# Products of P and V issued as two column halves of 64 queries by turns, and eight constants moved to another PSUM bank

## The chip, the cores and the metric

One core of a Trainium2 chip runs one program. Its engines work side by side and wait for each other by semaphores: TensorE (PE; its weight loads are listed apart as PEld), VectorE (DVE), ScalarE (ACT), GpSimd (POOL) and SyncE (SP), which issues most transfers. The metric is the device time of one execution in microseconds; lower is better.

## What is computed

Attention that keeps the 32 largest scores of each query, then a routed feed-forward layer with 8 experts, then a dense one with g = h cos(h). Cut to what matters here:

```python
# q, k, v: (4, 8, 576, 64) fp32
scores = np.matmul(q, k.transpose(0, 1, 3, 2)) / np.sqrt(D)
kth = np.partition(scores, -32, axis=-1)[..., -32:-31]
scores = np.where(scores >= kth, scores, -1e9)
attn = np.exp(scores - scores.max(-1, keepdims=True))
attn = attn / (attn.sum(-1, keepdims=True) + 1e-9)
x = np.matmul(attn, v)                      # the products of P and V
x = x.transpose(0, 2, 1, 3).reshape(2304, 512)
x = moe(x)      # top tokens of each expert by capacity 288, relu(x w1) w2
out = (h * cos(h)) @ w_out                  # h = x @ w_in
```

## The kernel before

Attention is 144 tiles of 128 queries by 576 keys: for each of 16 pairs of heads, four full tiles of each head and a ninth tile (`hs == 2`) that holds the last 64 queries of both heads. Four tiles are a group; there are 36 groups. `run` is a software pipeline written out by hand: in `step`, group gA = step gets its scores (`qk_mm` on PE, `qk_ev` on ACT writes `S`), gB its largest values by chunks (`chunks`, `thresh` on DVE), gC its sign count and exponentials (`sign_exp` on ACT: `sg`, `E`) and the product `W` (`below` on POOL), gD its 32nd largest score (`kth` on DVE) and the masked exponentials `P` (`probs`, on DVE, ACT and POOL by a pattern of four letters), gE the transposes of P (`tr`, `tr_tail` on PE; copies `PT` and `PTt` on ACT), gF the products with V (`av`), gG the division (`fin` on DVE). Each engine does its instructions in the order in which this loop writes them; a letter `u` counts the four tiles of a group.

`kth` takes the eight largest of `W` and picks the one whose rank was counted: four instructions a step (`oh`, L241) that compare the count with `R8`, eight constants for all partitions that stand in PSUM. `tr_tail` (L283) transposes the last 64 keys of two tiles into `ptail`, and one ACT copy a group (L293, `PTt`) takes them out. In `tight` steps, the last ones, copies and products come one tile at a time.

`av` computes out[queries, 65] = P^T-blocks times V with a column of ones: four blocks of 128 keys (L308) and one of the last 64 keys, which are stored for two heads together (L309). The stationary operand is the transposed P, 128 keys by 128 queries; what streams are the 65 columns of V. In fp32 the chip shows two instructions for each product. In ordinary steps `av` is called for two tiles when u = 2 and for two when u = 3; this is called a visit below. For the ninth tile it already computes two halves of 64 queries, all of the first and then all of the second.

The eight PSUM banks hold two `sp` tiles of two banks, two `pt`, one `av` and one `ptail`. Before, the bank `av` is one tile for the whole stage (`B2`); it holds the products (columns 0 to 259) and `R8` (260 to 267). Waits are set by tile: whoever touches a tile waits for the others who touched it before.

After attention comes the routing search, then the gathers, the two feed-forward layers and the stores.

Of the kernel before, what the change touches and what calls it, by code (L numbers as in the profile page):

```python
# [9 lines left out]
F32 = mybir.dt.float32  # L10
# [83 lines left out]
def head_tiles():  # L94
    t = []
    for p in range(NP):
        for s in range(2):
            for i in range(4):
                t.append((p, s, i))
        t.append((p, 2, 4))  # L100
    return t
# [11 lines left out]
class Attention:  # L113
# [4 lines left out]
    def __init__(s, k, sb, ps, slow=False):  # L118
        s.k, s.nc, s.sb, s.ps, s.slow = k, k.nc, sb, ps, slow
        s.tiles = head_tiles()  # L120
        s.nsp, s.ntail = (1, 2) if slow else (2, 1)
        G = s.nc.gpsimd

        s.B2 = ps.tile([128, 512], F32, name="av")
        s.R8 = s.B2[:, 260:268]
        s.nc.vector.tensor_copy(s.R8, k.rank8)

        s.XB, s.XT = {0: s.x_tile()}, {0: s.x_tile(0)}
        s.NV = 2 if slow else 6
        s.VM = [sb.tile([128, 2, 4, 65], F32, name=f"vm{i}") for i in range(s.NV)]  # L130
        s.VT = [sb.tile([128, 2, 2, 65], F32, name=f"vt{i}") for i in range(s.NV)]
        for t in s.VM:
            G.memset(t[:, :, :, 64:65], 1.0)
        for t in s.VT:
            for z in range(2):
                G.memset(t[64 * z:64 * z + 64, z, :, 64:65], 1.0)
                G.memset(t[64 * (1 - z):64 * (1 - z) + 64, z], 0.0)
        s.QZ = []
        for i in range(1 if slow else PLACES):
            z = [sb.tile([128, 512], F32, name=f"qz{i}{a}") for a in range(2)] + [sb.tile([128, 128], F32, name=f"qm{i}")]  # L140
            G.memset(z[0][64:128, :], 0.0)
            G.memset(z[1][0:64, :], 0.0)
            G.memset(z[2][0:64, 64:128], 0.0)
            G.memset(z[2][64:128, 0:64], 0.0)
            s.QZ.append(z)
        s.QT, s.KT, s.SP, s.SS, s.CC, s.TB, s.NMX, s.SUM, s.M3 = ({} for _ in range(9))
        s.todo, s.turned = [], []
        s.SG, s.EX, s.W, s.TB2, s.PB, s.PT, s.PTL, s.PTS, s.AVP = ({} for _ in range(9))
# [130 lines left out]
    def tr_tail(s, j):  # L279
        g, u = divmod(j, 4)  # L280
        if u == 1:
            s.PTL[g] = s.ps.tile([128, 2, 128], F32, name="ptail", bufs=s.ntail)
        s.nc.tensor.transpose(s.PTL[g][:, u // 2, :], s.PB[j // 2][:, 512:640], s.k.ident)  # L283

    def tr_ev(s, j):
# [9 lines left out]
    def av(s, j, two=False):  # L295
        PEe = s.nc.tensor
        g, u = divmod(j, 4)
        p, hs, i = s.tiles[j]
        t, tt = s.values(p)
        if u == 0:  # L300
            if two and g % 2 == 0:
                s.AVP[g] = s.ps.tile([128, 2, 512], F32, name="sp", bufs=s.nsp)[:, 0, :260].rearrange("p (a b) -> p a b", a=4)
            else:
                s.AVP[g] = s.B2[:, :260].rearrange("p (a b) -> p a b", a=4)
        o = s.AVP[g]
        for a, lo, hi in (((hs, 0, 128),) if hs < 2 else ((0, 0, 64), (1, 64, 128))):
            for c in range(4):
                PEe.matmul(o[lo:hi, u, :], s.PT[j][:, c * 128 + lo:c * 128 + hi], t[:, a, c, :], start=c == 0, stop=False)  # L308
            PEe.matmul(o[lo:hi, u, :], s.PTS[g][:, u // 2, lo:hi], tt[:, j % 2, a, :], start=False, stop=True)  # L309

    def fin(s, g, ends):
# [1232 lines left out]
```

## Time and profile before

| | |
|---|---|
| median of 3 runs | 1247.97 us (1246.42 to 1253.18) |
| the profiled execution | 1246.51 us, its span 1244.7 us |
| PE busy | 1131.7 us, 91% of the span |
| DVE busy | 1058.9 us, 85% |
| ACT busy | 787.8 us, 63% |
| POOL busy | 603.3 us, 48% |
| mean granted TensorE clock | 0.948 of full speed |

Busy time is the time in which an engine had an instruction under way. Matmuls are pipelined, so a busy PE is not PE at its peak. A row of a timeline gives the start in us from the span's start, the time until the end of the last instruction in the row, the engine, the line, what is written and read, the shapes (for PE first the rows and columns of the array in use), the count, and in brackets the idle time before it and who ended it.

### The profile page before, as it was taken

How to read it: one execution, taken by the hardware profiler on the slowest of the kernel's cores; microseconds unless marked ns; L12 is line 12 of the kernel's file. 1: busy time of each engine (PE TensorE's matmuls, PEld its weight loads, DVE VectorE, ACT ScalarE, POOL GpSimd, SP SyncE). 2: the span in 40 equal slices, each digit the busy share in tenths (PEclk: the TensorE clock that was granted, in tenths of full speed). 3: DMA queues.
4: the chain of work that ended last, by engine and by line, in shares of the span. 5: the costliest groups of instructions: out<-in, count | busy, mean ns of one | idle time of the engine just before them, and what ended most of it. 6: DMA issues, size and time to landing. Idle time of an engine off the chain costs nothing.

```text
span 1244.7 us, 22829 instructions
## 1 busy us (share of the span) xinstructions
PE 1131.7 (91%) x7449; PEld 996.6 (80%) x7449; DVE 1058.9 (85%) x4172; ACT 787.8 (63%) x1539; POOL 603.3 (48%) x592
## 2 busy tenths in 40 slices
PE   6799999999999986688898989989889999999996
PEld 4588787787878776578888889978777998999985
DVE  7999999999999984687888878699999668777774
ACT  6999989989998951333445446655655545444442
POOL 5999989989998960211000020164665343121120
PEclk9999999989998986698999989999898999999998
DMA  5111121121111001455555567522321100000000
GB/s 124 38 45 38 38 70 32 32 70 32 32 32 39 2 1 39 155 171 164 189 175 167 172 197 240 178 68 85 130 93 67 35 26 18 26 26 27 26 26 29
DMA packets 61890, 98.07 MB, mean 79 GB/s; under 512 B 30912, under 2 KB 30912, under 8 KB 61248
## 3 DMA queue, kind: packets, MB, share of 16 engines
q1 hardware_dynamic: 53648, 74.47, 19.6%
q10 hardware_dynamic: 5136, 12.60, 3.0%
q0 software_dynamic: 2976, 9.44, 2.3%
q8 instruction: 61, 1.00, 0.3%
q14 instruction: 69, 0.57, 0.1%
HBM read 78.66 MB, written 17.83 MB: 78 GB/s over the span
## 4 chain that ended last, share of the span: by engine, by line
PE 36%; DVE 32%; ACT 13%; issue 9%; POOL 5%; DMA 4%; POOLq 0%; DVEq 0%; SPq 0%; ACTq 0%
PE pa L1326 10%; PE y L1374 10%; DVE C L195 5%; PE pa L1174 4%; PE y L1189 4%; ACT sg L226 4%; DMA row<-x,i 3%; DVE w L244 3%; ACT E L228 3%; ACT S L189 2%; DVE wu L1256 2%; PE sp L185 2%; ACT PT L287 2%; PE av L308 2%; DVE ct L1334 2%
## 5 line engine op out<-in xcount | busy, mean ns | idle before, releaser
L1326 PE MATMUL pa<-yh,wu 128*128 128x384 f32 x1152 | 222.3, 340 | 10.7 <-POOL yh L1310 4.8
L1374 PE MATMUL y<-wu,gh 128*128 128x512 f32 x864 | 222.7, 402 | 5.6 <-POOL gh L1362 4.9
L1326 PEld LDWEIGHTS pa<-yh,wu 128*128 128x128 f32 x1152 | 206.0, 189 | 22.4 <-POOL yh L1310 6.4
L232 POOL TENSOR_TENSOR W<-sg,S 128x576 f32<-128x576 bf16 x144 | 197.8, 1379 | 33.0 <-ACT sg L226 31.6
L1374 PEld LDWEIGHTS y<-wu,gh 128*128 128x128 f32 x864 | 164.2, 192 | 38.9 <-POOL gh L1362 6.5
L185 PE MATMUL sp<-kT,qz 128*128 128x288 f32 x512 | 175.7, 433 | 12.7 <-ACT S L189 7.4
L195 DVE MAX8 C<-S 128x8 f32<-128x72 f32 x1152 | 162.5, 215 | 6.5 <-ACT S L189 6.3
L308 PE MATMUL av<-vm,PT 128*128 128x65 f32 (+1 forms) x1216 | 150.5, 274 | 13.7 <-DVE xb L331 7.5
L308 PEld LDWEIGHTS av<-vm,PT 128*128 128x128 f32 (+1 forms) x1216 | 139.1, 190 | 20.4 <-DVE xb L331 11.4
L1358 ACT ACTIVATE gh<-cx 128x384 fp32r<-128x384 f32 x95 | 49.9, 525 | 143.4 <-DVE cx L1356 140.9
L1151 POOL DMA_INDIRECT row<-x,i x24 | 29.5, 1231 | 215.9 <-DVE hh L1181 34.4
L269 POOL TENSOR_TENSOR P<-sg,E 128x576 f32<-128x576 bf16 x102 | 131.4, 1288 | 3.8
L1174 PE MATMUL pa<-xh,wu 128*128 128x288 f32 x768 | 124.9, 314 | 0.0
L277 PEld LDWEIGHTS pt<-ident,P 128*128 128x128 f32 x576 | 80.2, 145 | 52.7 <-POOL P L269 11.5
L1189 PE MATMUL y<-hh,wu 128*128 128x288 f32 x768 | 120.1, 306 | 0.0
L277 PE MATMUL pt<-ident,P 128*128 128x128 f32 x576 | 110.7, 279 | 6.0 <-POOL P L269 4.6
L1174 PEld LDWEIGHTS pa<-xh,wu 128*128 128x128 f32 x768 | 112.1, 201 | 3.2 <-issue 2.9
L226 ACT ACTIVATE sg<-S,tb 128x576 bf16<-128x576 f32 x144 | 111.7, 775 | 1.2
L228 ACT ACTIVATE E<-S,nmx 128x576 f32<-128x576 f32 x144 | 110.8, 769 | 0.0
L1189 PEld LDWEIGHTS y<-hh,wu 128*128 128x128 f32 x768 | 109.2, 196 | 1.7 <-ACT hh L1180 0.8
L189 ACT ACTIVATE S<-sp 128x576 f32<-128x576 f32 x144 | 92.5, 642 | 27.8 <-PE sp L185 27.7
L244 DVE MAX8 w<-W 128x8 f32<-128x576 f32 x144 | 104.6, 746 | 1.3 <-POOL W L232 1.2
(243 smaller groups left out, 2149.8 us busy)
## 6 DMA issues: line engine op xcount, KB each, us to landing
raw<-in_moe_w_dram SPq DMA_DIRECT2D x63, 512.0 KB, 3.9
kT<-in_k_dram SPq DMA_DIRECT2D x16, 288.0 KB, 3.2
qz<-in_q_dram SPq DMA_DIRECT2D x32, 128.0 KB, 3.2
vm<-in_v_dram SPq DMA_DIRECT2D x32, 128.0 KB, 3.0
x<-xb SPq DMA_DIRECT2D x4, 1024.0 KB, 4.1
r<-in_moe_w_in_dram ACTq DMA_DIRECT2D x8, 512.0 KB, 4.9
r<-in_moe_w_out_dram ACTq DMA_DIRECT2D x8, 512.0 KB, 5.0
half<-in_moe_w_in_dram SPq DMA_DIRECT2D x8, 512.0 KB, 3.7
```

The lines of the kernel that those rows point to most:

```text
L185: s.nc.tensor.matmul(s.SP[j][:, c, :288], lh, s.KT[p][:, o + c * 288:o + c * 288 + 288], start=True, stop=True)
L195: s.nc.vector.max(c[:, e, :], s.SS[j][:, 72 * e:72 * e + 72])
L226: A.activation(s.SG[j], s.SS[j], AF.Sign, bias=s.TB[g][:, u:u + 1], scale=-EPS1, accum_out=s.SUM[g][:, u:u + 1])
L228: A.activation(s.EX[j], s.SS[j], AF.Exp, bias=s.NMX[g][:, u:u + 1])
L232: s.nc.gpsimd.tensor_tensor(s.W[j], s.SG.pop(j), s.SS[j], op=OP.mult)
L244: V.max(w8[:, u, :], s.W.pop(4 * g + u))
L277: s.nc.tensor.transpose(s.PT[j][:, i * 128:(i + 1) * 128], s.PB[j // 2][:, o + i * 128:o + (i + 1) * 128], s.k.ident)
L308: PEe.matmul(o[lo:hi, u, :], s.PT[j][:, c * 128 + lo:c * 128 + hi], t[:, a, c, :], start=c == 0, stop=False)
L1174: PEe.matmul(p, w[:, a, f * 128:(f + 1) * 128], XH[e, c][:, b, :], start=n == 0, stop=n == 11)
L1189: PEe.matmul(Y[e][m], w[:, a, o + m * 128:o + (m + 1) * 128], t[:, b, :], start=f == 0 and i == 0, stop=f == 7 and i == 2)
L1326: s.nc.tensor.matmul(p, w[:, a, f * 128:(f + 1) * 128], s.YH[q, c][:, b, :], start=n == 0, stop=n == 11)
L1374: PEe.matmul(O[q][m], g[:, a, m * 128:(m + 1) * 128], w[:, b, c:c + 512], start=first and j == 0, stop=last and j == 2)
```

## The change

Every tile's products are now issued as two halves of 64 queries (columns of the stationary operand), by turns: block c of the first half, block c of the second, then block c + 1. The ninth tile, whose halves belong to two heads, gets the same order. The products get a tile of their own from the pool (`av`), and `R8` moves to a tile for the whole stage (`B1`) that also holds the transposes of the last keys (`ptail`, columns 0 to 255). The count of banks is the same.

```diff
-        s.nsp, s.ntail = (1, 2) if slow else (2, 1)
+        s.nsp = 1 if slow else 2
...
-        s.B2 = ps.tile([128, 512], F32, name="av")
-        s.R8 = s.B2[:, 260:268]
+        s.B1 = ps.tile([128, 512], F32, name="ptail")
+        s.R8 = s.B1[:, 256:264]
...
         if u == 1:
-            s.PTL[g] = s.ps.tile([128, 2, 128], F32, name="ptail", bufs=s.ntail)
+            s.PTL[g] = s.B1[:, :256].rearrange("p (a b) -> p a b", a=2)
...
             else:
-                s.AVP[g] = s.B2[:, :260].rearrange("p (a b) -> p a b", a=4)
+                s.AVP[g] = s.ps.tile([128, 4, 65], F32, name="av")
         o = s.AVP[g]
-        for a, lo, hi in (((hs, 0, 128),) if hs < 2 else ((0, 0, 64), (1, 64, 128))):
-            for c in range(4):
+
+        halves = tuple((hs if hs < 2 else z, 64 * z, 64 * z + 64) for z in range(2))
+        for c in range(4):
+            for a, lo, hi in halves:
                 PEe.matmul(o[lo:hi, u, :], s.PT[j][:, c * 128 + lo:c * 128 + hi], t[:, a, c, :], start=c == 0, stop=False)
+        for a, lo, hi in halves:
             PEe.matmul(o[lo:hi, u, :], s.PTS[g][:, u // 2, lo:hi], tt[:, j % 2, a, :], start=False, stop=True)
```

The program's order on PE in an ordinary step, third tile of a group (u = 2), before. The number behind a tensor's name is one of its buffers; the brackets name the engines waited for.

```order
L283 MATMUL ptail<-ident,P 128x128 [waits Activation_49]
L185 MATMUL sp<-kT,qz_177 128x288 [waits Activation_49]
L277 MATMUL pt<-ident,P 128x128 [waits Activation_49,Pool_49]
L277 MATMUL pt<-ident,P 128x128
L185 MATMUL sp<-kT,qz_177 128x288
L277 MATMUL pt<-ident,P 128x128 x2
L308 MATMUL av<-vm_129,PT 128x65 [waits DVE_49]
L308 MATMUL av<-vm_129,PT 128x65 x3
L309 MATMUL av<-vt_135,PTt 128x65
L308 MATMUL av<-vm_129,PT 128x65 x4
L309 MATMUL av<-vt_135,PTt 128x65
```

The same place after the change.

```order
L283 MATMUL ptail<-ident,P 128x128 [waits DVE_49,Activation_49]
L185 MATMUL sp<-kT,qz_177 128x288 [waits Activation_49]
L277 MATMUL pt<-ident,P 128x128 [waits Activation_49,Pool_49]
L277 MATMUL pt<-ident,P 128x128
L185 MATMUL sp<-kT,qz_177 128x288
L277 MATMUL pt<-ident,P 128x128 x2
L310 MATMUL av<-vm_129,PT 64x65 [waits DVE_49]
L310 MATMUL av<-vm_129,PT 64x65 x7
L312 MATMUL av<-vt_135,PTt 64x65 x2
L310 MATMUL av<-vm_129,PT 64x65 x8
L312 MATMUL av<-vt_135,PTt 64x65 x2
```

The transpose of the last keys now waits for DVE as well (the picks of the same step), and each product stands there twice, for 64 queries each.

On DVE, the start of a step (`kth` of one group with `fin` of another), before.

```order
L244 MAX w_6698<-W 128x8 [waits Pool_49] x2
L241 SCALAR_TENSOR_TENSOR oh,tall<-av,sum,w_6698 128x8 [waits DVE_49,PE_49,Activation_49]
L244 MAX w_6698<-W 128x8 [waits Pool_49]
L241 SCALAR_TENSOR_TENSOR oh,tall<-av,sum,w_6698 128x8 [waits DVE_49,Activation_49]
L244 MAX w_6698<-W 128x8 [waits Pool_49]
L241 SCALAR_TENSOR_TENSOR oh,tall<-av,sum,w_6698 128x8 [waits DVE_49,Activation_49]
L315 TENSOR_SCALAR rinv<-av 128x4
```

And after.

```order
L244 MAX w_7217<-W 128x8 [waits Pool_49] x2
L241 SCALAR_TENSOR_TENSOR oh,tall<-ptail,sum,w_7217 128x8 [waits DVE_49,Activation_49]
L244 MAX w_7217<-W 128x8 [waits Pool_49]
L241 SCALAR_TENSOR_TENSOR oh,tall<-ptail,sum,w_7217 128x8 [waits DVE_49]
L244 MAX w_7217<-W 128x8 [waits Pool_49]
L241 SCALAR_TENSOR_TENSOR oh,tall<-ptail,sum,w_7217 128x8 [waits DVE_49]
L318 TENSOR_SCALAR rinv<-av 128x4 [waits PE_49]
```

The first pick waited for PE's products of the step before; now it waits for ACT, whose last copy from that bank is `PTt` of the step before. The wait for PE's products stands at the division (`rinv`).

On PE near the end of attention, where the tile `hs == 2` of group 33 is computed, before.

```order
L277 MATMUL pt<-ident,P 128x128 x3
L308 MATMUL av<-vm_129,PT 64x65 [waits DVE_49]
L308 MATMUL av<-vm_129,PT 64x65 x3
L309 MATMUL av<-vt_135,PTt 64x65 [waits Activation_49]
L308 MATMUL av<-vm_129,PT 64x65 x4
L309 MATMUL av<-vt_135,PTt 64x65
L277 MATMUL pt<-ident,P 128x128 [waits PE_49]
L277 MATMUL pt<-ident,P 128x128 x3
L283 MATMUL ptail<-ident,P 128x128 [waits PE_49]
```

And after.

```order
L277 MATMUL pt<-ident,P 128x128 x3
L310 MATMUL av<-vm_129,PT 64x65 x8
L312 MATMUL av<-vt_135,PTt 64x65 [waits Activation_49]
L312 MATMUL av<-vt_135,PTt 64x65
L277 MATMUL pt<-ident,P 128x128 [waits DVE_49,PE_49]
L277 MATMUL pt<-ident,P 128x128 x3
L283 MATMUL ptail<-ident,P 128x128 [waits DVE_49]
```

The product's wait for DVE is gone, and the transpose of the last keys has one.

## Rows read from the trace of the kernel before

**Rows 1.** Busy time of each engine, its share of the span, instructions (the page).
```profile
PE 1131.7 (91%) x7449; PEld 996.6 (80%) x7449; DVE 1058.9 (85%) x4172; ACT 787.8 (63%) x1539; POOL 603.3 (48%) x592
```

**Rows 2.** Windows: length, busy PE, PEld, DVE, ACT, POOL (instructions), clock, DMA, GB/s.
```profile
30.00:450.00 420.00, 396.42 (x2796) 333.27 (x2797) 411.97 (x2671) 398.58 (x824) 385.59 (x341) 0.97 0.13 37
450.00:487.00 37.00, 29.78 (x225) 27.86 (x224) 18.49 (x60) 10.13 (x22) 4.95 (x4) 0.77 0.09 33
487.00:1245.00 758.00, 684.31 (x4360) 622.98 (x4360) 606.48 (x1287) 359.74 (x659) 196.13 (x182) 0.94 0.32 102
```

**Rows 3.** What DVE waited for from 30 to 450 us: total us, times, longest.
```profile
DVE oh L241 <- PE av L309: 3.2, 3, 1.2
DVE L L390 <- PE pt L385: 1.5, 3, 0.5
```

**Rows 4.** PE's timeline, a visit of two full tiles in step 8.
```profile
85.92 1.11 PE L308 MATMUL av<-vm,PT 128*128 128x65 f32 x8 [0.95 <-DVE xb L331]
...
88.20 0.46 PE L185 MATMUL sp<-kT,qm 128*128 128x288 f32 x1
```

**Rows 5.** PE's timeline in step 21.
```profile
246.22 0.27 PE L283 MATMUL ptail<-ident,P 128*128 128x128 f32 x1
...
248.28 1.11 PE L308 MATMUL av<-vm,PT 128*128 128x65 f32 x8 [0.37 <-DVE xb L331]
```

**Rows 6.** PE's timeline, a tile in two halves behind a full tile.
```profile
99.12 0.39 PE L309 MATMUL av<-vt,PTt 128*128 128x65 f32 x2
99.43 0.74 PE L308 MATMUL av<-vm,PT 128*64 128x65 f32 x10
99.95 0.22 PE L309 MATMUL av<-vt,PTt 128*64 128x65 f32 x1
...
100.57 0.61 PE L385 MATMUL pt<-wg,xT 128*128 128x8 f32 x4
```

**Rows 7.** PE's timeline, small products of the routing search.
```profile
488.79 0.61 PE L787 MATMUL pa<-rO,yh 128*24 128x8 bf16 x18 [2.13 <-DVE yh L759]
```

**Rows 8.** DVE's timeline in step 21: the last pick, the last division.
```profile
246.89 0.08 DVE L241 DVE_READ_ACCUMULATOR oh<-av,sum,w 128x1 f32 x1
...
248.00 0.23 DVE L331 TENSOR_TENSOR xb<-av,rinv 128x64 f32<-128x64 f32 x1
```

**Rows 9.** ACT's timeline in step 21: the third tile's scores.
```profile
250.60 0.64 ACT L189 ACTIVATE S<-sp 128x576 f32<-128x576 f32 x1
```

**Rows 10.** ACT's timeline at the end of step 14.
```profile
171.69 0.40 ACT L293 ACTIVATE PTt<-ptail 128x256 f32<-128x256 f32 x1
```

**Rows 11.** DVE's timeline there.
```profile
169.74 0.23 DVE L241 SCALAR_TENSOR_TENSOR oh<-av,sum,w 128x8 f32<-128x8 f32 x1
...
172.00 0.76 DVE L244 MAX8 w<-W 128x8 f32<-128x576 f32 x1 [1.22 <-POOL W L232]
```

**Rows 12.** What ACT waited for from 30 to 450 us.
```profile
ACT S L189 <- PE sp L185: 18.4, 12, 4.0
```

**Rows 13.** Windows (columns as in rows 2) at a lower granted clock.
```profile
152.50:159.30 6.80, 6.80 (x39) 6.04 (x38) 5.91 (x40) 3.31 (x7) 6.19 (x6) 0.50 0.02 5
...
456.30:463.10 6.80, 4.41 (x32) 4.29 (x33) 5.09 (x18) 0.77 (x2) 0.22 (x1) 0.50 0.00 1
```

**Rows 14.** PE's timeline in the tail.
```profile
458.69 1.19 PE L308 MATMUL av<-vm,PT 128*64 128x65 f32 x10 [5.22 <-DVE oh L241]
...
461.58 0.42 PE L283 MATMUL ptail<-ident,P 128*128 128x128 f32 x1
...
476.24 1.54 PE L308 MATMUL av<-vm,PT 128*128 128x65 f32 x8
...
480.13 2.19 PE L385 MATMUL pt<-wg,xT 128*128 128x8 f32 x10
```

**Rows 15.** DVE's timeline in the tail: the last pick.
```profile
458.56 0.07 DVE L241 DVE_READ_ACCUMULATOR oh<-av,sum,w 128x1 f32 x1
```

**Rows 16.** The products P on DVE, 90 to 450 us: shortest, median, longest in ns.
```profile
L262 DVE SCALAR_TENSOR_TENSOR P<-S,tall,E x30: 797/919/1891, 99.1 to 450.0; 128x576 f32<-128x576 f32 x30
```

## The prediction

> **What bounds the kernel now.** I began with the busy times of the page [rows 1]. No engine stands out: TensorE (PE) 91%, VectorE (DVE) 85%. Shares over a whole span hide stages, so the next view is the table of windows [rows 2]. Attention runs from 30 to 450 us, then its tail to about 487 us, then the two feed-forward layers. The diff touches attention alone. The reader is to see that from 30 to 450 us DVE is busy 411.97 of 420 us. PE reads 396.42 us, and ScalarE and GpSimd are nearly as full. So in the long middle, whatever PE saves, the time can fall by no more than DVE's 8.0 idle us, unless DVE's own work gets shorter. In the tail DVE is busy 18.49 of 37 us and PE 29.78: there PE's order sets the end.
>
> Next come DVE's waits in that middle stretch [rows 3]: 3.2 us in three waits of the rank pick (`oh`, L241) for the P and V products, and 1.5 us in three waits of `L` for PE's logits. These are what a faster PE could give back; the rest of the 8 us is in small pieces.
>
> **What a P-V product costs now.** The PE timeline shows one visit to the P-V products [rows 4]: two tiles of 128 queries, 20 instructions, begin at 85.92 and the next scores at 88.20 us. That is 2.28 us, 0.114 each. There are 36 groups of four tiles with two visits each. A step (one group) lasts about 12.5 us: the first products of step 8 begin at 85.92, those of step 21 at 248.28 [rows 4, 5], so 162.36 / 13 = 12.49.
>
> The trace already holds the shape that the change uses: the tile of the last 64 queries of two heads is done today in halves of 64 columns, one half after the other [rows 6]. Its 20 instructions begin at 99.43 us and the next product at 100.57: 1.14 us, half of 2.28. And where the second half follows the first they run together: at 99.95 us the first half's L309 and the second half's L308 lie in the same stretch. A half product then takes a slot of about 57 ns, 1.14 us / 20, and the two halves need not share slots.
>
> **Halves by turns.** If each pair of halves shares a slot, a tile is 10 slots instead of 20 instructions of 0.114. The 64-column tile had about 17 slots, because three pairs overlapped (20 less 3), in 1.14 us; that includes the change of shape on the way in and out. Seven slots fewer are 1.14 - 7 x 0.057 = 0.74 us for a lone tile, and a second tile in the same visit adds 10 x 0.057 = 0.57. The way in costs more than the slots show: L309 began at 99.12 with two instructions of 0.114, so the next was due at 99.35 and came at 99.43, 0.08 later. A visit is then about 0.74 + 0.57 + 0.08 = 1.39 us against 2.28: 0.89 us less. Bounds: nothing saved if the halves exclude each other (40 slots of 0.057 = 2.28, and 0.08 more), 0.9 saved at best. I take 0.85, since the overlap is in the trace. From 30 to 450 us some 60 visits stand, so PE loses about 51 us of 396. DVE's work stays, so nearly all of that turns into PE idle time.
>
> The Trainium skill, "TensorEngine Tiling (Array Packing)", Key Properties, says that changing the tiling mode drains the engine; the trace agrees with 0.08 us. The skill's "TensorE: Matmul & The Clock Gate", section on the 56 ns gap, says that with hardware decoding off the sequencer spends about 62 ns on each matmul. By that two tiles would take 40 x 62 = 2.48 us, 0.2 more than now, and the change would lose. Rows speak against that here: 18 small products, with their weight loads, took 0.61 us in all, under 34 ns each [rows 7].
>
> **The constants.** Four picks a step read `R8`. It stood in the bank of the products and stands now in the bank of the last keys' transposes. So the three DVE waits for L309, 3.2 us, go. In their place two waits come, as the order shows. The first pick waits for the copy of the transposes (PTt, ScalarE), and the step's first tail transpose on PE waits for the last pick.
>
> The second costs PE something each step. At step 21 the transpose ran at 246.22 and the picks ended only at 246.97 [rows 5, 8]: 0.75 us of waiting, with the scores and transposes of the third tile queued behind it. Who waits for those? ScalarE copies that tile's scores at 250.60 [rows 9]. PE needs about 1.4 us from the transpose to these scores, so they would be ready at 246.97 + 1.4 = 248.4, over 2 us early. It is also largely the old wait moved: PE stood still before the products anyway until DVE had freed their bank (248.00, products at 248.28). So I cost it at nothing in the middle; if ScalarE moved more than 2 us ahead against DVE the cover would be gone.
>
> The first wait can cost DVE. After step 14 the pick began at 169.74 us, while the copy ended at 171.69 + 0.40 = 172.09 [rows 10, 11]: 2.35 us late. Why is ScalarE late there? Its copies of scores waited for PE 12 times, 18.4 us in all, up to 4.0 us [rows 12]. The long waits are at the places where the granted clock is 0.50, the lower level of 1.2 GHz; one is 152.5 to 159.3 us [rows 13]. There the first visits took twice as long. With halves by turns PE is about 1.5 us sooner through such a place, so the wait would be nearer 0.9 us; DVE's 1.22 us wait for W in the same step [rows 11] then shrinks too. Three such places before 450 us: -3.2 (picks) - 1.5 (logits) - 2 (W) + 3 (new waits) = about -3.5 us, bounds +3 and -8.
>
> **The tail.** At 453.5 us PE stops for 5.22 us, released by the picks [rows 14]: the next product writes the bank they read, and DVE has P products to finish first. The picks end at 458.63 [rows 15]. After the change this product no longer waits for the picks, nor do the transposes behind it. But the tail transpose does: it ran at 461.58 and would run at about 458.65. The stall stays, and 2.9 us of work move ahead of it. Behind it PE has nine more tiles until 480.13, seven of them alone in their visit. A lone tile saves 1.14 - 0.82 = 0.32 us, seven 2.2; the two at 476.24 take 3.89 us today, much of it at the lower clock [rows 14], and by turns some 2.7: 1.2. Sum 6.3. The lower clock of 456.3 to 463.1 us [rows 13] would now cover more of the work, which I cost at 1 us. Tail: -5 us, bounds -2 and -7. What follows (routing, gathers, feed-forward) starts that much earlier.
>
> **Sum.** -3.5 - 5 = -8.5 us. The profiled execution took 1246.51 us, 1.8 more than its span and 1.5 less than the median of the runs, 1247.97. From the median: 1239.5 us.
>
> **Rivals.**
> *No measurable change*, 1242 to 1253. DVE holds the middle, the new wait for the copy eats what the old one gave, and the tail gains only 2 or 3 us. For it: 412 of 420. Against it: 5.22 us in one place with 2.9 movable. Chance 0.32.
> *More than forecast*, 1225 to 1233. DVE's products P (L262) take from 797 to 1891 ns, median 919 [rows 16]; what stretches them is where they meet GpSimd's work. The 30 rows would be 3.7 us shorter at 0.797 than at the median alone, more for the long ones. With ScalarE and GpSimd earlier against DVE these meetings fall otherwise, in either sense. The skill's "SBUF — State Buffer", on who interferes with whom, says that such a two-input product and a GpSimd operation block each other whole. Chance 0.13.
> *Slower, by the clock*, 1256 to 1290. PE has 51 us more idle time in the middle. The granted clock falls to 0.50 in three stretches of 6.8 us there, although PE is then hardly idle. If it fell in each of the 34 steps, ScalarE would be up to 4 us late every time and DVE about 1.2 us: 30 x 1.2 = 36 us, less 8.5. It decides from about eight more falls. Against it: the falls of before came while PE was hardly idle, so idle time is not what these rows show ahead of a fall. Chance 0.10.
> *Halves that don't overlap*, by the 62 ns or otherwise: PE gets 60 x 0.1 to 0.3 = 6 to 18 us more, and DVE's slack takes about half; 1247 to 1257. Chance 0.05.
>
> **Numbers.** The forecast, 1234 to 1242, has 0.40. Under 0.5% (6.2 us), about what can be told from no change here, means 1241.7 to 1254.2. Faster: 0.40 + 0.13, and 0.02 from the edge of the second case. Same: 0.30 of the second and 0.04 of the last two. Slower: 0.11. The range leaves out the ends of both outer cases: 1229 to 1252.
>
> **What would show it.** Visits of two tiles near 1.4 us, with half products in pairs that start within a few ns, show the first step. PE's busy time between 30 and 450 us some 50 us lower with DVE's still above 97% of the stretch shows that DVE binds. The tail transpose waiting for L241 near 453 us, in place of the product, shows the moved stall. Wrong would be: halves in single file, DVE waiting for PTt by more than 1 us in most steps, more than six stretches at 0.50 before 450 us, or a DVE busy time that moves by over 8 us.

## The result and the profile after

The changed kernel took 1231.44 us (median of 4 runs, 1228.86 to 1235.91), the kernel before beside it 1250.58 (4 runs, 1246.42 to 1253.49): ratio 0.9853, 95% interval 0.9807 to 0.9900. Two later measurements gave 0.9924 (0.9875 to 0.9974) and 0.9868 (0.9817 to 0.9919). So it is faster, by 0.8 to 1.5%. Every ratio here is taken over the executions in the faster of the two states in which executions come, so it is not the quotient of the medians beside it. The forecast was 1239.5; the time lies inside the range, but under the likeliest case (1234 to 1242).

Busy time on the page after answers to [rows 1].

```profile
PE 1065.6 (87%) x8729; PEld 916.9 (75%) x8729; DVE 1058.5 (86%) x4172; ACT 789.3 (64%) x1539; POOL 604.4 (49%) x592
```

The windows after answer to [rows 2]. From 30 to 450 us PE is busy 50.4 us less, DVE 5.1 us more.

```profile
30.00:450.00 420.00, 346.05 (x4015) 269.96 (x4015) 417.03 (x2674) 403.36 (x830) 391.63 (x343) 0.97 0.14 37
450.00:487.00 37.00, 22.59 (x366) 18.54 (x362) 23.44 (x101) 7.45 (x15) 1.11 (x5) 0.82 0.10 35
```

DVE's waits from 30 to 450 us, after (total us, times, longest). The picks' three waits of [rows 3] are gone and none for PTt has come.

```profile
DVE L L393 <- PE pt L388: 0.9, 2, 0.4
```

PE's waits in the same stretch. The time that PE no longer works it stands at the tail transpose (L283) until the picks are through; the profile names the reciprocal that follows the last pick.

```profile
PE ptail L283 <- DVE rinv L320: 51.2, 28, 3.5
PE ptail L283 <- DVE oh L241: 10.6, 3, 4.1
```

PE's timeline, a visit of two full tiles after (in place of [rows 4]): from 87.53 to the next scores at 88.84, 1.31 us, where it was 2.28.

```profile
87.53 0.69 PE L310 MATMUL av<-vm,PT 128*64 128x65 f32 x16
88.05 0.29 PE L312 MATMUL av<-vt,PTt 128*64 128x65 f32 x4
88.16 0.64 PE L310 MATMUL av<-vm,PT 128*64 128x65 f32 x16
88.63 0.29 PE L312 MATMUL av<-vt,PTt 128*64 128x65 f32 x4
88.84 0.75 PE L185 MATMUL sp<-kT,qm 128*128 128x288 f32 x2
```

Two marks on DVE divide the span. The last pick ended at 458.63 us before and ends at 454.35 now (-4.3). The last logits ended at 486.69 + 0.38 = 487.07 and end at 472.39 + 0.39 = 472.78; so the tail between the two marks went from 28.44 to 18.43 us (-10.0). DVE's timeline at that second mark, before and after:

```profile
486.69 0.38 DVE L390 TENSOR_TENSOR L<-L,pt 128x32 f32<-128x32 f32 x2 [3.95 <-PE pt L385]
```

```profile
472.39 0.39 DVE L393 TENSOR_TENSOR L<-L,pt 128x32 f32<-128x32 f32 x2 [2.02 <-PE pt L388]
```

What follows took 757.6 us before and 754.2 after (-3.4). Its program is the same, and a second profile of the kernel before gave 753.4, a third of the change 757.9. So those 3.4 us lie within what one kernel shows against itself, and I do not count them as the change's: about 14 are.

### The profile page after: what moved, and what is told of

It is laid out like the page before. It is cut to its first block, busy times and chain, and to the rows that moved or that the text cites. A ratio compares the mean times of both kernels' runs of the same rounds, so it can differ in the third digit from the quotient of the medians.

```text
span 1227.0 us, 25337 instructions
## 1 busy us (share of the span) xinstructions
PE 1065.6 (87%) x8729; PEld 916.9 (75%) x8729; DVE 1058.5 (86%) x4172; ACT 789.3 (64%) x1539; POOL 604.4 (49%) x592
## 4 chain that ended last, share of the span: by engine, by line
DVE 51%; PE 32%; issue 9%; DMA 4%; POOL 2%; ACT 2%; POOLq 0%; DVEq 0%; SPq 0%; ACTq 0%
DVE C L195 11%; PE pa L1329 10%; PE y L1377 10%; DVE w L244 6%; PE pa L1177 4%; PE y L1192 4%; DVE P L262 3%; DMA row<-x,i 3%; DVE wu L1259 3%; DVE C L212 2%; DVE oh L241 2%; DVE ct L1337 2%; DVE C L206 2%; DVE row L1113 2%; PE sp L185 1%
## 5 line engine op out<-in xcount | busy, mean ns | idle before, releaser
L269 POOL TENSOR_TENSOR P<-sg,E 128x576 f32<-128x576 bf16 x102 | 137.2, 1345 | 3.3
L1154 POOL DMA_INDIRECT row<-x,i x24 | 29.3, 1220 | 213.3 <-issue 34.7
L1177 PE MATMUL pa<-xh,wu 128*128 128x288 f32 x768 | 121.4, 308 | 0.0
L1177 PEld LDWEIGHTS pa<-xh,wu 128*128 128x128 f32 x768 | 108.9, 195 | 3.2 <-issue 2.9
L244 DVE MAX8 w<-W 128x8 f32<-128x576 f32 x144 | 104.7, 747 | 0.1
L1336 DVE TENSOR_SCALAR ct<-pa 128x384 f32<-128x384 f32 x95 | 52.7, 555 | 59.3 <-PE pa L1329 59.2
L185 PEld LDWEIGHTS sp<-kT,qz 128*128 128x128 f32 x512 | 81.1, 196 | 21.6 <-ACT S L189 8.1
```

The source lines that it names most:

```text
L185: s.nc.tensor.matmul(s.SP[j][:, c, :288], lh, s.KT[p][:, o + c * 288:o + c * 288 + 288], start=True, stop=True)
L244: V.max(w8[:, u, :], s.W.pop(4 * g + u))
L269: nc.gpsimd.tensor_tensor(P, m, s.EX[j], op=OP.mult)
L1177: PEe.matmul(p, w[:, a, f * 128:(f + 1) * 128], XH[e, c][:, b, :], start=n == 0, stop=n == 11)
```

## The experiments

For the middle I compare the same 29 steps in every version, from the first `w` (L244) of group 3 to that of group 32. DVE does the same work in them everywhere except for the products P (L262), which meet GpSimd. The windows of these steps and the group of P (count, total us, mean ns), before:

```profile
57.87:419.29 361.42, 345.53 (x2453) 292.69 (x2452) 353.64 (x2298) 342.03 (x705) 328.03 (x290) 0.97 0.14 40
```

```profile
L262 DVE SCALAR_TENSOR_TENSOR P<-S,tall,E 128x576 f32<-128x576 f32 x29 | 33.8, 1166 | 0.0
```

The same of after:

```profile
58.00:414.09 356.09, 300.71 (x3499) 236.19 (x3498) 353.37 (x2298) 345.48 (x711) 331.60 (x291) 0.98 0.15 41
```

```profile
L262 DVE SCALAR_TENSOR_TENSOR P<-S,tall,E 128x576 f32<-128x576 f32 x29 | 33.8, 1166 | 0.0
```

DVE busy less P is 319.8 and 319.6 us. In all versions of the table it lies between 319.3 and 320.5 (for the constants in SBUF, after the longer picks are taken off). So the middle is read as 320 + P + DVE's idle time (length less busy time). All columns are us, except the clock and the ratio with its 95% interval.

| version | 29 steps | DVE idle | P | PE busy | clock | tail | time | ratio to before |
|---|---|---|---|---|---|---|---|---|
| before | 361.4 | 7.8 | 33.8 | 345.5 | 0.97 | 28.4 | 1250.6 | |
| before, again | 360.0 | 7.1 | 32.9 | 345.0 | 0.97 | 28.4 | 1240.8 | one run |
| full change | 356.1 | 2.7 | 33.8 | 300.7 | 0.98 | 18.4 | 1231.4 | 0.9853 [0.9807, 0.9900] |
| full change, again | 356.1 | 2.7 | 33.9 | 300.7 | 0.98 | 18.4 | 1232.3 | 0.9924 [0.9875, 0.9974] |
| full change, third | 355.1 | 3.0 | 32.3 | 301.0 | 0.97 | 18.4 | 1231.5 | 0.9868 [0.9817, 0.9919] |
| turns only | 350.8 | 2.0 | 29.5 | 301.0 | 0.98 | 21.4 | 1228.4 | 0.9903 [0.9875, 0.9931] |
| constants only | 363.1 | 6.3 | 36.4 | 335.3 | 1.00 | 36.7 | 1258.8 | 1.0148 [1.0119, 1.0176] |
| halves in file | 366.1 | 9.0 | 36.8 | 335.5 | 0.98 | 27.6 | 1240.6 | 0.9960 [0.9923, 0.9996] |
| later tail transposes | 363.0 | 3.9 | 39.6 | 304.1 | 0.95 | 18.4 | 1238.8 | 0.9967 [0.9942, 0.9991] |
| constants in SBUF | 386.9 | 1.8 | 44.1 | 317.3 | 0.92 | 17.2 | 1267.4 | 1.0209 [1.0150, 1.0267] |
| fewer products | 362.6 | 3.7 | 38.8 | 286.7 | 0.90 | 20.8 | 1234.6 | one run |
| turns in tail only | 358.2 | 5.1 | 33.4 | 341.8 | 0.98 | 21.7 | 1237.8 | 0.9914 [0.9878, 0.9950] |
| turns in middle only | 351.0 | 2.3 | 29.3 | 299.7 | 0.98 | 28.4 | 1234.7 | 0.9880 [0.9834, 0.9925] |
| turns, last picks from SBUF | 350.9 | 2.0 | 29.5 | 301.0 | 0.98 | 17.1 | 1221.1 | 0.9787 [0.9738, 0.9835] |

Each ratio is to runs of the kernel before on the same chip: median 1247.8 us beside *full change, again*, *turns only*, *constants only* and *halves in file*; 1244.2 beside *before, again* and the three from *later tail transposes* on; 1249.8 beside *full change, third* and the last three. *Turns in middle only* spread most, from 1223.9 to 1253.7.

**Each part alone.** *Turns only*: the kernel before with the new loop of products; `R8` stays in their bank.

```diff
-        for a, lo, hi in (((hs, 0, 128),) if hs < 2 else ((0, 0, 64), (1, 64, 128))):
-            for c in range(4):
+        halves = tuple((hs if hs < 2 else z, 64 * z, 64 * z + 64) for z in range(2))
+        for c in range(4):
+            for a, lo, hi in halves:
...
+        for a, lo, hi in halves:
...
```

> Halves by turns, constants left in the bank of the products. Theory A (the shorter products give the middle and part of the tail, the moved constants let 2.9 us of work pass ahead of the stall): a visit of two tiles stays at 1.3 to 1.4 us, the 5.2 us stall of PE on the picks near 453 us comes back, the middle gains 3 to 5 us, and the whole is 8 to 13 us faster than before, 4 to 8 us slower than the full change. Rival B (the constants give most of the gain): within 4 us of before. Rival C (the gain is the granted clock in the tail): no steady difference to the full change; it goes with the number of stretches at 0.50 after 440 us.

*Constants only*: the full change with the old loop of products.

> Constants moved, products as before (128 columns). Theory A: PE waits in each step at the tail transposes for the picks with products of 2.28 us behind them, so its slack in the middle is used up: between 4 us faster and 5 us slower than before. Rival B: 10 us faster or more.

*The full change again*, unchanged.

> The full change once more on the chip of the other three, for its time beside theirs and a second profile. Theory A: attention ends 12 to 15 us earlier than in the profile of before, with DVE busy over 98% of 30 to 440 us. Rival C: the end of attention moves by 4 us or more with the place where the clock falls in the tail.

The turns alone carry the gain. Of the 10.6 us that they take off the 29 steps (361.4 to 350.8), 5.8 are idle time of DVE and 4.3 are P. The groups of P and of the picks, turns only, and then the picks before:

```profile
L262 DVE SCALAR_TENSOR_TENSOR P<-S,tall,E 128x576 f32<-128x576 f32 x29 | 29.5, 1016 | 0.0
L241 DVE SCALAR_TENSOR_TENSOR oh<-av,sum,w 128x8 f32<-128x8 f32 x116 | 24.1, 208 | 0.2
```

```profile
L241 DVE SCALAR_TENSOR_TENSOR oh<-av,sum,w 128x8 f32<-128x8 f32 x116 | 24.2, 209 | 3.4 <-PE av L309 3.2
```

So the picks stop waiting for the products although `R8` still stands in the products' bank: the shorter products end that wait, not the move of the constants. The constants alone make the kernel slower: DVE waited 2.7 us for PTt in six places, and its tail ran at the lower clock from end to end (0.50 in the window of the tail) and took 36.7 us; its 29 steps, at 1.00, were 1.7 us longer than before. Put beside the turns, the constants cost 5.2 us in the middle (350.8 to 356.1, of which P 4.3) and give 3.0 back in the tail (21.4 to 18.4). I had the turns alone 4 to 8 us behind the full change: wrong. The full change again ended attention 14.2 us ahead of before (472.84 to 487.07 us), as Theory A had it. The tail's 3.0 goes with the moved stall, as PE's timeline shows, turns only and then the full change:

```profile
446.84 1.14 PE L309 MATMUL av<-vm,PT 128*64 128x65 f32 x16 [6.06 <-DVE oh L241]
```

```profile
454.40 0.33 PE L283 MATMUL ptail<-ident,P 128*128 128x128 f32 x1 [1.62 <-DVE oh L241]
```

With turns only the work behind the stall also runs at the lower clock until 450.9 us, while in the full change that lower stretch (442.9 to 449.8) is over ahead of the last pick. How much of the 3.0 is the clock no run separates.

**By turns, or one after the other.** The full change with the order of loops exchanged; the same instructions.

```diff
-        for c in range(4):
-            for a, lo, hi in halves:
+        for a, lo, hi in halves:
+            for c in range(4):
...
-        for a, lo, hi in halves:
...
```

> The full change, but each tile's first half wholly before its second half. Theory A (halves share slots only where they meet in the queue, about three pairs at each border): a visit of two tiles takes about 31 slots of 57 ns and 0.2, so 1.9 to 2.0 us; the time lies between before and the full change, 5 to 12 us faster than before. A rival by which order does not matter (the engine pairs halves by itself): a visit of 1.4 us and the time of the full change.

PE's timeline there: the visit begins at 87.54 and the next scores at 89.49, 1.95 us; in turns the same 40 products took 1.31.

```profile
87.54 0.74 PE L310 MATMUL av<-vm,PT 128*64 128x65 f32 x10
88.06 0.22 PE L311 MATMUL av<-vt,PTt 128*64 128x65 f32 x1
88.11 0.22 PE L310 MATMUL av<-vm,PT 128*64 128x65 f32 x1
...
89.28 0.28 PE L311 MATMUL av<-vt,PTt 128*64 128x65 f32 x2
89.49 0.75 PE L185 MATMUL sp<-kT,qm 128*128 128x288 f32 x2
```

So a half product costs 33 ns by turns and 49 ns in file (1.31 and 1.95 us by 40), and the rival, that order does not matter, is out. Its profiled execution took 1250.4 us, 9.8 above the median of its runs, so its middle is not weighed. By its ratio it lies between before and the full change.

**Does DVE bind the middle?** The full change with one block of 128 keys in place of four.

```diff
-        for c in range(4):
+        for c in range(1):
```

> The full change, leaving out three of the four blocks of 128 keys of the products of P and V (the output is that of the last block and the last 64 keys' only). Theory (DVE binds the middle): PE's busy time from 30 to 450 us falls by another 40 to 60 us, and the 29 ordinary steps shrink by no more than 5 us; the tail shrinks by up to 6 us. Rival (PE still sets part of the middle's time): the 29 steps shrink by 10 to 40 us.

Its 29 steps and its P:

```profile
56.24:418.86 362.62, 286.68 (x2111) 211.34 (x2110) 358.92 (x2298) 346.42 (x713) 331.58 (x292) 0.90 0.14 40
```

```profile
L262 DVE SCALAR_TENSOR_TENSOR P<-S,tall,E 128x576 f32<-128x576 f32 x29 | 38.8, 1339 | 0.0
```

A visit fell to 0.62 us (87.60 to 88.22). The steps did not shrink: they are 6.5 us longer than the full change's, 5.0 of it P and 1.0 idle time. So the theory holds in that PE's work is not what the steps wait for; that P would grow it had not. From 30 to 450 us PE's busy time fell by 19 us (346.05 to 327.24), not 40 to 60, and in the steps by 14: the granted clock, 0.98 in the full change, is 0.90, and the same transposes and scores take longer. Of DVE's waiting, 1.0 us is for PTt. Whether the lower clock also has a part in the longer P is not shown.

**The stall at L283.** The full change with the tail transposes one or two tiles later.

```diff
-                    if u % 2:
-                        s.tr_tail(4 * gE + u)
+                    tails = {2: (1,), 3: (3,)} if tight else {3: (1, 3)}
+                    for w in tails.get(u, ()):
+                        s.tr_tail(4 * gE + w)
```

> The full change, but the transposes of the last keys are issued one or two tiles later in each step, so that PE does not stand at L283 until the picks are through. Theory (that hold sets how P falls against GpSimd, and the stall in the tail can be filled): the waits of L283 for the picks shrink to under a third, the 29 ordinary steps take 350 to 353 us on DVE as in the version with the turns only, the tail stays near 18 us, and the time is 3 to 8 us below the full change. Rival 1 (how P meets GpSimd is not set by this hold): the 29 steps stay at 355 to 357 us and the time within 3 us of the full change. Rival 2 (the copy PTt is now late for the products and the next pick): DVE waits for PTt by over 0.5 us a step and the time is 5 to 15 us above.

The wait left L283 and went to the products, as PE's waits from 30 to 450 us show:

```profile
PE av L310 <- DVE xb L334: 43.0, 24, 3.6
```

DVE idled 1.1 us more and P took 5.8 more. So P is long without a hold at L283 too. Neither the theory nor a rival held: the steps took 363.0 us, not 350 to 353 or 355 to 357, and DVE waited for PTt 2.0 us in all, not 0.5 a step.

**The constants in SBUF.** The full change with `s.R8 = k.rank8`.

> The full change, with the eight constants read from SBUF and no copy of them in PSUM. Theory (a pick with two SBUF inputs can be held up by GpSimd's work as P is): the 144 picks become 0.2 to 1 us longer, DVE's busy time rises by 20 us or more, and the time goes up by 20 to 60 us; the stall in the tail before L283 is gone, -3 us. Rival (eight columns are too short to be held up): the picks keep their 0.1 to 0.2 us, PE waits no more for picks, and the time is 0 to 8 us below the full change.

The 116 picks of the 29 steps, this version:

```profile
L240 DVE SCALAR_TENSOR_TENSOR oh<-rank,sum,w 128x8 f32<-128x8 f32 x116 | 45.5, 392 | 0.0
```

The same picks in the full change:

```profile
L241 DVE SCALAR_TENSOR_TENSOR oh<-ptail,sum,w 128x8 f32<-128x8 f32 x116 | 24.2, 209 | 0.2
```

That is 21.3 us more, and P took 10.3 more. Most picks stayed short (the median is 210 ns), some were held for up to 1348. So the theory held, and the constants' place in PSUM is worth keeping here.

**The kernel before, again**, to see whether its clock falls where it fell.

> The kernel before, profiled a second time. Theory (where the granted clock falls follows from the order of the work): the lower clock covers the same stretches near 456 to 463 us and from 476 us on, and the tail from the last pick to the last logits takes 28 to 29 us again. Rival (the falls come where they like): the lower clock lies elsewhere and the tail takes anything from 20 to 37 us; then the tail's gain of 10 us is in part chance.

The tail took 28.44 us, with the lower clock from 2.5 us ahead of the last pick (2.3 in the first profile) and again from 18.0 us behind it (18.1). So in the tail the place belongs to the kernel, and the theory held. In the middle it does not: lower stretches began at 311.2 and 348.8 us, where the first profile has none.

**Tail and middle apart.** Turns only, in one of the two stretches: the new loop stands under the condition, the loop of before under `else`. `two` is true in the tight steps; the second version has `not two`.

```diff
+        if two:
...
+        else:
...
```

> The kernel before, with the halves by turns in the tight steps only (groups 32 to 35); the middle and the place of the constants are those of before. Theory (the tail's gain is mostly the lower clock that does not cover it): the middle takes 360 to 362 us for the 29 steps as before, the fall of the clock stays where it was, 2.4 us ahead of the last pick, the stall of 5 us before the products stays, and the tail gives back only 2 to 4 of the 28.4 us; the time is 0 to 4 us below before. Rival (the shorter visits alone make the tail): the tail takes 19 to 22 us with the fall at its old place; 7 to 9 us below before.

> The kernel before, with the halves by turns up to group 31 only; the tail's products are whole tiles again. Theory: the 29 steps take 351 to 357 us as with turns everywhere, the clock's fall lies elsewhere against the last pick, and the tail takes 23 to 26 us, since half of its gain is the clock; the time is 7 to 12 us below before. Rival (the tail's gain is its own shorter visits): the tail takes 28 us; 4 to 8 us below before.

I had put the tail's unforeseen gain down to a fall of the clock that no longer covers it because the middle is earlier. That theory fell. With turns in the tail alone the first fall stays at its place (from 2.2 us ahead of the last pick) and the tail takes 21.65 us; with turns in the middle alone it takes 28.43. So both rivals held for the tail; by their ratios the times are 11 and 15 us below before, more than any of the forecasts. Windows of the kernel before: the stretch at full clock ahead of the second fall, then the tail, split where its last two tiles begin:

```profile
463.10:476.70 13.60, 12.75 (x114) 12.35 (x114) 4.86 (x25) 4.38 (x10) 0.00 (x0) 1.00 0.00 1
458.63:476.24 17.61, 16.70 (x140) 16.18 (x140) 7.63 (x32) 4.85 (x11) 0.22 (x1) 0.87 0.00 1
476.24:487.07 10.83, 9.61 (x56) 8.69 (x55) 2.30 (x12) 1.30 (x2) 0.00 (x0) 0.52 0.30 110
```

The tail's two stretches with turns in the tail only:

```profile
454.57:470.31 15.74, 14.83 (x210) 12.44 (x211) 7.64 (x32) 4.85 (x11) 0.22 (x1) 0.85 0.01 2
470.31:476.22 5.91, 4.69 (x66) 4.12 (x65) 2.32 (x12) 1.30 (x2) 0.00 (x0) 1.00 0.45 174
```

Up to the last two tiles the turns give 1.87 us. Behind that, 10.83 us at clock 0.52 became 5.91 at 1.00: 4.92 us. An estimate: a visit of two tiles at full clock saves 0.97 us (2.28 to 1.31), so about 4 of the 4.92 are the clock. The second fall did not go away: it begins at 476.3, as attention ends, instead of 10 us ahead of its end. With whole tiles in the tail (before, twice, and turns in middle only) the fall began 10.2 to 10.4 us ahead of attention's end, with halves of all products within 1.1 us of it. Three profiles show that this is not the whole rule: *constants only* stood at 0.50 throughout; in *halves in file* the first lower stretch covers half of the tail (460.8 to 474.5 us), which took 27.6 us; and with *fewer products* the second fall came 5.1 us ahead of the end.

**A version that beats both.** Turns only, with the picks of the last two groups reading SBUF, where GpSimd has hardly any work left.

```diff
+        R8 = k.rank8 if g >= 34 else s.R8
...
-            V.scalar_tensor_tensor(oh[:, u, :], s.R8, s.SUM[g][:, u:u + 1], w8[:, u, :], op0=OP.is_equal, op1=OP.mult, accum_out=T[:, u:u + 1])
+            V.scalar_tensor_tensor(oh[:, u, :], R8, s.SUM[g][:, u:u + 1], w8[:, u, :], op0=OP.is_equal, op1=OP.mult, accum_out=T[:, u:u + 1])
```

> Halves by turns everywhere, the constants in the products' bank for the groups up to 33, and read from SBUF by the picks of the last two groups, where GpSimd has little to do. Theory: the 29 steps as with the turns only (350 to 353 us), no product and no transposition of the tail waits for a pick, the picks of the last two groups stay under 0.25 us, the tail takes 17 to 18.5 us instead of 21.4, and the time is 2 to 4 us below both the full change and the turns only. Rival (the stall goes on elsewhere: P, which comes after the picks on DVE, is what the tail waits for): the tail stays at 20 to 22 us, no change against the turns only.

> The full change once more, to stand beside the other three: theory and rival alike expect 8 to 16 us below before, the 29 steps near 356 us and the tail near 18.4 us. If the profile shows the 29 steps at 362 us or more, then how the products P fall against GpSimd is not a matter of the kernel's order but of the execution.

The full change came out as expected (29 steps of 355.1 us, a tail of 18.4, about 16 us below before by its ratio). The new version took 1221.1 us (1219.88 to 1223.65) where the full change beside it took 1231.47 (1227.12 to 1235.51): 10 us less, where 2 to 4 had been forecast. Its middle is that of the turns only; its picks stay short and hold nothing, and the whole tail runs at full clock. DVE's timeline of the last pick, and the window of the tail:

```profile
446.88 0.21 DVE L242 SCALAR_TENSOR_TENSOR oh<-rank,sum,w 128x8 f32<-128x8 f32 x1
447.02 0.08 DVE L242 DVE_READ_ACCUMULATOR oh<-rank,sum,w 128x1 f32 x1
```

```profile
447.10:464.15 17.05, 11.73 (x181) 9.68 (x176) 9.86 (x44) 4.25 (x10) 0.22 (x1) 1.00 0.16 63
```

Attention ends 5.7 us before the full change's in that measurement (464.15 to 469.85). *Turns only* ran on another chip, at 1228.4 us; its attention ended at 468.17, 4.0 us later. The rest of the span is 4.2 us shorter too (753.7 to 757.9), the difference that the kernel before also showed against itself. Of the 9.9 us between the two spans, 5.7 are explained; whether the rest belongs to the version stays open.

## Why the prediction was right, and where its size was off

**DVE binds the middle: right.** PE's busy time from 30 to 450 us was forecast 51 us lower and is 50.4 lower; DVE's share rose to 99%. In the 29 steps the net gain is DVE's idle time, 7.8 to 2.7 us, with P at 33.8 in both. But P is equal only because two effects cancel: the turns alone brought it down to 29.5, and the constants brought it back. Taking still more work from PE did not shorten the steps.

**The visit: right.** 1.39 us was forecast, 1.31 measured, and 1.95 in file; the 0.97 saved lie a little above the 0.9 that was to be the best. The 40 products with their weight loads in 1.31 us are 33 ns each. So the 62 ns a matmul that the Trainium skill gives for hardware decoding switched off ("TensorE: Matmul & The Clock Gate", section on the 56 ns gap) do not bind them. A lone tile in the tail takes 0.73 us instead of 1.06, but the four transposes ahead of it 0.59 instead of 0.44: the change of shape costs 0.15 us there, which the forecast had only for the way in. PE's timeline at one, before and then with turns in the tail only:

```profile
467.81 0.61 PE L277 MATMUL pt<-ident,P 128*128 128x128 f32 x4
468.25 1.00 PE L308 MATMUL sp<-vm,PT 128*128 128x65 f32 x8
469.09 0.39 PE L309 MATMUL sp<-vt,PTt 128*128 128x65 f32 x2
469.31 0.61 PE L277 MATMUL pt<-ident,P 128*128 128x128 f32 x4
```

```profile
462.77 0.65 PE L277 MATMUL pt<-ident,P 128*128 128x128 f32 x4
463.36 0.69 PE L310 MATMUL sp<-vm,PT 128*64 128x65 f32 x16
463.88 0.29 PE L312 MATMUL sp<-vt,PTt 128*64 128x65 f32 x4
464.09 0.66 PE L277 MATMUL pt<-ident,P 128*128 128x128 f32 x4
```

**The constants in the middle: the sum near, its reasons wrong.** Forecast -3.5, measured -5.3 in the 29 steps and -4.3 at the last pick. The picks' 3.2 us went, but the prediction credited that to the constants' move: with the turns alone they go as well, and with the constants alone 2.7 us for PTt take their place. The 3 us set against them for PTt did not come beside the turns (no such wait in the first profile, 0.2 us in the third). The move itself cost 5.2 us there, 4.3 of them P, where the forecast had its two waits cancel and the hold at L283 at nothing. That moving the constants causes this is shown (P of 32.3 to 33.9 us in three profiles with them moved, 29.3 to 29.5 in three without); by which step it shifts GpSimd against DVE is not, but it does not need the hold at L283, since P grew further where that was gone. That -10.6 of the turns and +5.2 of the constants add up near the forecast is luck.

**The tail: the term that was mis-sized.** Forecast -5 (bounds -2 and -7), measured -10.0. The moved stall was 2.9 and gave 3.0 (near the end PE is held at L283 by the picks twice, 2.98 us until 443.6 and 1.62 until 454.4). The lone tiles were 2.2, and the stretch that holds them gave 1.87 net. The failing term is the last two tiles, 1.2: I left them, and the logits behind them, at the lower clock, and took 1 us off for the clock besides. They gave 4.92, most of it because the second fall now comes as attention ends. 1.87 + 4.92 + 3.0 = 9.8 of the 10.0.

**The rivals.** *More than forecast* has the time (1225 to 1233), and P took the same 33.8 us; its cause is at work even so, since with the turns alone P fell by 4.3. *Slower by the clock* stood on 1.2 us of DVE for each further fall. One sign of being wrong did come: the clock stood at 0.50 in seven stretches between 30 and 450 us (from 50.4, 74.3, 193.8, 231.3, 258.6, 309.8 and 442.9 us), where the prediction set the mark at more than six. But they cover 27 us in all, as the five before did, and DVE's idle time in the steps is 2.7 us. With fewer products the lower clock covers far more of the steps (0.90 in place of 0.98) and DVE's idle time is 3.7 us: by its waits, a fall cost DVE far less than 1.2 us each, though P took 5.0 us more in that run. My argument there, that idle time is not what stands ahead of a fall, is weakened by the same run. *No change* and *no overlap* did not come.

## What to carry to other kernels

Where an engine that does not bind gets faster, first count the binding engine's idle time, then ask which of its own instructions the new order will lengthen or shorten: with the turns alone the 29 steps fell by 10.6 us, more than the 7.8 idle ones. Look for the rest at the ends, where the order of work or the clock decides. Two products on different columns of the array were worth issuing in alternation (33 ns each), not one after the other (49). Try each part of a change alone: here one part carried the gain, and the other's purpose was better met by reading the constants from SBUF for the last two groups alone.

## What the runs showed of the hardware

**P against GpSimd** is the largest swing in the middle: 29.3 to 39.6 us for the same 29 products among the versions with the constants in PSUM, 797 ns each at best [rows 16]. Turns only, DVE's and then GpSimd's timeline at a P that begins just ahead of GpSimd's W:

```profile
365.63 0.80 DVE L262 SCALAR_TENSOR_TENSOR P<-S,tall,E 128x576 f32<-128x576 f32 x1
```

```profile
364.19 1.29 POOL L269 TENSOR_TENSOR P<-sg,E 128x576 f32<-128x576 bf16 x1
365.42 0.18 POOL L215 COPY tall<-m 128x4 f32<-128x4 f32 x1
365.58 0.22 POOL L251 TENSOR_SCALAR tb<-tall 128x4 f32<-128x4 f32 x1
365.77 3.06 POOL L232 TENSOR_TENSOR W<-sg,S 128x576 f32<-128x576 bf16 x2
```

Here P keeps its 0.80 us, and the two W behind it take 3.06 us, where two took 2.54 in the rows below. In the full change, at a P that begins behind a W:

```profile
258.95 1.82 DVE L262 SCALAR_TENSOR_TENSOR P<-S,tall,E 128x576 f32<-128x576 f32 x1
```

```profile
257.62 2.54 POOL L232 TENSOR_TENSOR W<-sg,S 128x576 f32<-128x576 bf16 x2
260.11 1.80 POOL L269 TENSOR_TENSOR P<-sg,E 128x576 f32<-128x576 bf16 x1
```

P began 1.2 us before GpSimd's second W ended (257.62 + 2.54 = 260.16) and ended 0.6 us after it; GpSimd's next product then took 1.80 us instead of 1.29. The Trainium skill, "SBUF — State Buffer", section on who interferes with whom, has the two block each other whole; these rows agree, and the picks that read SBUF (392 ns on average in place of 209) do too.

**The clock's fall near the end of attention** followed the shape of PE's work. In the kernel before PE was busy 12.75 of the 13.60 us at full clock ahead of the fall at 476.7. With turns in the tail only the full clock lasted 17.0 us (459.3 to 476.3); with halves in file it lasted 13.6 again (474.5 to 488.1). What in the whole tiles brings that fall on, and why the halves by turns put it off, stays open.
